# Taking the dummy products out between the last four modes of a spectral-mixing kernel

## Chip, cores, metric

One core of a Trainium2 chip. The metric is the device time of one execution in microseconds (us). All timed runs below count as fast in the record. Where runs of one kernel are called long, they are the longer ones among these.

## The reference

Sliding-window causal attention, then a spectral mix of its output along the sequence, then a channel product with a rectifier:

```python
attn_out = _attn_ref(q, k, v)               # 8 batches, 8 heads, 576 rows, 64 wide, window 64
X = np.fft.rfft(x, axis=1)                  # x: (8, 576, 512)
Yr = einsum(Xr, w_r) - einsum(Xi, w_i)      # 64 modes, a 512x512 matrix for each
Yi = einsum(Xr, w_i) + einsum(Xi, w_r)
y = np.fft.irfft(Y, n=S, axis=1)
u = x + y
out = u + np.maximum(u @ w_ch, 0.0)
```

The weights w_r and w_i, 128 matrices of 512x512, are most of what is read.

## The kernel before

The weights stream in, one matrix (512 KB as bf16) every 2.45 us, and TensorE multiplies each as it lands. The last four modes (ME = 60 to 63) are done in a narrow form, `last`, 16 columns wide. Their result `psl` is copied, turned into rows (`turned`: four 512-column products and four transposes), and then the 36 output tiles are made: `lay(n)` puts a first product into the bank of tile n, `rectify(n)` adds a second and applies the rectifier on ScalarE, `finish(n)` adds the third and hands the tile to VectorE. Between the last groups stand dummy products, `idle`, into a bank that nobody reads:

```python
def idle(wide, n):
    psd = ps_a.tile([128, DM], FP32, name="psd", tag="psw")
    for _ in range(wide):        # fp32 128x512: two products in the trace (x10 for five)
        nc.tensor.matmul(out=psd, lhsT=ident_r.bitcast(FP32), rhs=Z0[:, 0, :].bitcast(FP32), start=True, stop=True)
    for _ in range(5 * n):       # bf16, 96 columns
        nc.tensor.matmul(out=psd[:, 0:96], lhsT=ident_bf, rhs=view(x_sb, 0, [[1, 96]]), start=True, stop=True)

def last_mode(m, w, im, c0, c1):             # 16 weight loads, 16 products of 16 columns
    for c in range(c0, c1):
        for e in range(NC):
            nc.tensor.matmul(out=view(psl, ...), lhsT=w[:, c, 128*e:128*e+128], rhs=xq(c, m, im, ...), ...)

# ... (TensorE in program order)
last(ME + 1, 0)
for n in range(2, EARLY_ROWS):
    lay(n)
idle(1, 0)
last(ME + 1, 1)
for m in range(ME + 2, NM):
    for im in range(2):
        idle(1, 2)
        last(m, im)
idle(0, 2)
# ... the turn of the last rows
nc.vector.tensor_copy(out=view(YT2, ...), in_=view(psl, ...))
nc.vector.tensor_copy(out=YT2[:, :, 2 * R:], in_=psl[:, :, 2 * RL:])
turned(lambda e: YT2[:, e, 0:NR], NR, psa, psw)
lay(EARLY_ROWS)
# ... copies of psa and psw; then rectify(n), finish(n), lay(n) for 36 tiles, stores
turn_of = {1: 3, 5: 4, 9: 5, 12: 6, 15: 7}   # when the late rows of a batch are sent (Y <- yl)
```

The softmax here doesn't subtract the row's maximum and nothing guards it: scores larger than these inputs give would overflow.

## Time and profile before

| | before |
|---|---|
| time, median of the first 3 runs | 426.87 us (426.59 to 426.88) |
| span of the profiled run | 424.8 us |
| last group of narrow products starts | 390.05 us |
| turn of the last rows, four 512-column products | 1.17 us |
| first store of output issued | 396.81 us |
| TensorE clock in the seam, 380 to 395 us | 1.00 |

All places in time are us from the start of the span. The weights' DMA sets the time up to 390 us; then comes a short serial seam; the first output leaves at 397 us, and from 398 us the output runs with DMA, TensorE and ScalarE full and VectorE nearly so (400 to 410 us: DMA 0.98, the engines 10.00, 10.00 and 9.36 us busy). The prediction shows the lines. In them PE is TensorE, PEld its weight loads, DVE VectorE, ACT ScalarE and POOL GpSimd; L724 is line 724 of the kernel, and x4 counts instructions.

### The profile page before, as it was taken

To read this page: it belongs to the slowest core of one execution; us is meant where nothing else is said; L and a number is where in the kernel's file an instruction comes from. 1 tells how busy PE (TensorE), PEld (TensorE's weight loads), DVE (VectorE), ACT (ScalarE), POOL (GpSimd) and SP (SyncE) were. 2 spreads that over 40 slices of the span, in tenths; PEclk is the share of its full clock that TensorE was granted. 3 is DMA by queue.
4 is the path that set the end of the run, shared out by engine and by line. 5 is a ranking of instruction groups with operands and counts; after the bars stand their busy time and mean duration, and the time that the engine had idled before them with its cause. 6 is when DMAs were issued, how large, how long until landed. Compare 5 with 4: busy or idle time off the path is not lost.

```text
span 424.8 us, 8859 instructions
## 1 busy us (share of the span) xinstructions
PE 360.5 (85%) x3762; PEld 219.2 (52%) x3772; DVE 184.7 (43%) x397; ACT 171.4 (40%) x314; POOL 89.5 (21%) x171
## 2 busy tenths in 40 slices
PE   6989998998998899467698979999859886589993
PEld 5755765665665465222265646555334443256682
DVE  5566766766764201404542422333113432140994
ACT  4585765866863311201132313122113332130993
POOL 7231231331021141221221121121211032200000
PEclk9999999999995699965799998999999999999998
DMA  8999999999999999999999999999999999994598
GB/s 144 212 213 212 213 213 212 213 213 213 213 214 213 215 213 261 213 214 213 214 213 214 213 214 214 213 215 212 214 213 213 214 213 215 213 214 95 195 384 329
DMA packets 28646, 91.98 MB, mean 217 GB/s; under 512 B 2832, under 2 KB 3088, under 8 KB 28608
## 3 DMA queue, kind: packets, MB, share of 16 engines
q0 software_dynamic: 25344, 81.80, 96.6%
q1 hardware_dynamic: 3120, 9.50, 5.8%
q8 instruction: 29, 0.48, 0.4%
q10 hardware_dynamic: 144, 0.13, 0.1%
q14 instruction: 9, 0.07, 0.0%
HBM read 162.53 MB, written 9.44 MB: 405 GB/s over the span
## 4 chain that ended last, share of the span: by engine, by line
DMA 45%; PE 40%; DVE 8%; issue 2%; ACT 2%; POOL 1%; DVEq 0%; POOLq 0%
DMA wt<-in_moe_w_r_dram 32%; DMA wt<-in_moe_w_i_dram 9%; PE pso L316 7%; PE psy L575 7%; PE pst L218 6%; DMA wy<-in_moe_w_i_dram 5%; PE pso L885 4%; PE psv L235 3%; DVE x_sb L324 3%; PE psx L338 3%; PE pss L371 3%; PE pss L272 2%; PE pss L291 2%; DVE vT L59 2%; PE psw L724 1%
## 5 line engine op out<-in xcount | busy, mean ns | idle before, releaser
L575 PE MATMUL psy<-wt,XQ 128*32 128x512 bf16 (+1 forms) x404 | 96.6, 409 | 30.8 <-DMA wt<-in_moe_w_i_dram 15.5
L575 PEld LDWEIGHTS <-XQ 128*32 128x32 bf16 x476 | 48.6, 131 | 76.5 <-issue 57.0
L604 DVE CAST xT<-pxt 128x256 fp32r<-128x256 bf16 (+1 forms) x68 | 26.3, 434 | 53.8 <-PE pxt L597 34.1
L115 POOL DMA_DIRECT2D wt<-in_moe_w_r_dram x54 | 28.9, 536 | 92.2 <-DMA wt<-in_moe_w_r_dram 39.9
L611 ACT CAST Z<-psz 128x512 fp32r<-128x512 f32 x36 | 21.1, 586 | 66.6 <-PE psz L609 66.5
L115 POOL DMA_DIRECT2D wt<-in_moe_w_i_dram x52 | 28.0, 539 | 82.0 <-DMA wt<-in_moe_w_i_dram 43.7
L297 ACT ACTIVATE et<-pss 128x512 bf16<-128x512 f32 x72 | 39.2, 600 | 13.5 <-PE pss L291 13.4
L609 PE MATMUL psz<-wch,xT 128*128 128x512 f32 x144 | 42.4, 432 | 0.9 <-DVE xT L604 0.9
L316 PE MATMUL pso<-vt,et 128*64 128x65 bf16 (+1 forms) x576 | 34.3, 210 | 4.8 <-DVE x_sb L324 4.7
L609 PEld LDWEIGHTS psz<-wch,xT 128*128 128x128 f32 x144 | 27.1, 200 | 15.0 <-issue 8.7
L316 PEld LDWEIGHTS <-et 128*64 128x64 bf16 (+1 forms) x576 | 24.0, 114 | 17.1 <-issue 9.6
L59 DVE COPY x_sb<-psy 128x256 f32<-128x256 f32 x15 | 6.4, 424 | 56.7 <-PE psy L575 56.7
L324 DVE TENSOR_TENSOR x_sb<-pso,rcp 128x640 bf16<-128x640 f32 x32 | 26.3, 823 | 0.9
L58 ACT COPY x_sb<-psy 128x256 f32<-128x256 f32 x15 | 5.6, 373 | 50.2 <-DVE x_sb L59 50.2
L885 PE MATMUL pso<-Y,trigI 128*128 128x512 f32 x80 | 23.1, 402 | 0.1
L908 DVE TENSOR_TENSOR ot<-pso,x_sb 128x512 f32<-128x512 f32 x35 | 22.2, 685 | 1.5 <-PE pso L885 1.1
L272 PE MATMUL pss<-band,ident_bf 64*64 64x512 bf16 x136 | 20.6, 414 | 1.5 <-ACT et L297 1.5
L59 DVE CAST x_sb<-psj 128x512 bf16<-128x512 f32 x18 | 12.2, 688 | 21.3 <-PE psj L786 18.3
L59 DVE COPY vT<-pst 128x768 bf16<-128x768 bf16 x16 | 15.3, 958 | 13.0 <-PE pst L218 13.0
L890 ACT ACTIVATE pso<-pso 128x512 f32<-128x512 f32 x36 | 19.2, 597 | 0.0
L58 ACT CAST x_sb<-psj 128x512 bf16<-128x512 f32 x18 | 10.5, 585 | 19.6 <-PE psj L786 19.6
L291 PE MATMUL pss<-qT,kT 64*64 64x128 bf16 (+1 forms) x640 | 17.3, 221 | 0.3 <-issue 0.3
(157 smaller groups left out, 501.3 us busy)
## 6 DMA issues: line engine op xcount, KB each, us to landing
wt<-in_moe_w_r_dram POOLq DMA_DIRECT2D x54, 512.0 KB, 19.1
wt<-in_moe_w_i_dram POOLq DMA_DIRECT2D x52, 512.0 KB, 19.1
out_dram<-ot SPq DMA_DIRECT2D x15, 512.0 KB, 4.2
rk<-in_k_dram POOLq DMA_DIRECT2D x8, 576.0 KB, 9.7
rq<-in_q_dram POOLq DMA_DIRECT2D x8, 576.0 KB, 13.6
rv<-in_v_dram POOLq DMA_DIRECT2D x8, 576.0 KB, 12.3
wy<-in_moe_w_r_dram POOLq DMA_DIRECT2D x3, 512.0 KB, 17.7
wy<-in_moe_w_i_dram POOLq DMA_DIRECT2D x3, 512.0 KB, 19.1
```

Source lines behind the costliest of these rows:

```text
L59: return nc.vector.tensor_copy(out=o, in_=i)
L115: nc.gpsimd.dma_start(out=wt, in_=src[m].rearrange("(p c) e -> p c e", c=NC))
L218: nc.tensor.transpose(out=ps[64 * hh:64 * hh + 64, c, :], in_=src[:, hh, (c0 + c) * D:(c0 + c + 1) * D], identity=ident_bf)
L272: nc.tensor.matmul(out=pss[(2 * w + hh) % 3][64 * half:64 * half + 64, :], lhsT=ident_bf[pp, pp], rhs=view(band[pp], 128 * half, [[0, WIN ...
L291: nc.tensor.matmul(out=pss[(2 * w + hh) % 3][64 * half:64 * half + 64, col:col + nq], lhsT=kTs[b % 2][pp, g, 64 * kb:64 * kb + 64], rhs=qT ...
L297: nc.scalar.activation(out=et[:, hh, :], in_=pss[(2 * w + hh) % 3], func=ACT_F.Exp, scale=EX_SCALE)
L316: nc.tensor.matmul(out=pso[po, hh, (i // 2) * VW:(i // 2) * VW + D + 1], lhsT=et[pk, hh, col:col + 64], rhs=vt[pk, 1 - f % 2, 2 * hh + g / ...
L324: nc.vector.tensor_tensor(out=view(x_sb, b * NT * DM + g * D, [[4 * D, 2], [DM, NT], [1, D]]), in0=view(pso, 0, [[512, 2], [VW, NT], [1, D]]),
L575: nc.tensor.matmul(out=psy[r0:r0 + k, :], lhsT=xq(c, m, im, [[NM, k]]), rhs=w[:, c, :], start=(im + c == 0), stop=(im == (m > 0) and c == ...
L604: nc.vector.tensor_copy(out=xT[:, :, w * k:w * k + w], in_=view(psts[k], j, [[128, NC], [n, w]] if n > 1 else [[128, NC], [1, 64], [64, 2]]))
L609: nc.tensor.matmul(out=psz, lhsT=xT[:, c, :], rhs=wch[:, c, :], start=(c == 0), stop=(c == NC - 1))
L885: nc.tensor.matmul(out=tps[n], lhsT=trigI[:, tr:tr + 128], rhs=pair_tile(what, bb), start=False, stop=stop and r0 + k == 128, skip_group_c ...
```

## The change

Its intent, as the diff shows it: no dummy work between the last modes, as TensorE waits for weights there anyway, and only five small dummies where there were ten, in the turn.

```diff
         for n in range(2, EARLY_ROWS):
             lay(n)
-        idle(1, 0)
         last(ME + 1, 1)
         for m in range(ME + 2, NM):
             for im in range(2):
-                idle(1, 2)
                 last(m, im)
-        idle(0, 2)
+        idle(0, 1)
```

## The prediction

> **What bounds the kernel now.** I read the page first, for the rhythm of the whole run. The rows below have 40 slices of 10.6 us each. The first is the TensorE clock that was granted, the second the DMA share.

> ```profile
> PEclk9999999999995699965799998999999999999998
> DMA  8999999999999999999999999999999999994598
> ```

> The DMA engines are full until slice 36 (382 us); in that time the kernel loads weights, and TensorE has time to spare. Slices 37 and 38 (382 to 403 us) are the seam, where the weights are over and the output has not begun; after it the DMA is full again with output. A change in the seam can cost time, and this change lies just there. Next I read the chain of waits that ended last, in order of time (start, length, what):

> ```profile
> 370.83 19.17 DMA wy<-in_moe_w_i_dram
> 390.00 0.05 issue
> 390.05 0.67 PE psl L775 x16
> 390.71 0.02 issue
> 390.74 0.23 DVE YT L862
> 390.96 0.28 DVE YT L864
> 391.24 0.14 issue
> 391.37 1.17 PE psw L724 x4
> 392.54 0.02 issue
> 392.56 0.58 ACT Y L877
> 393.14 0.04 issue
> 393.19 2.19 PE pso L885 x7
> ```

> The last weights land at 390.00. From then on everything is in series: 16 narrow products of the last mode, two copies on VectorE, the turn of the last rows (four 512-column products), a copy on ScalarE, and then the output tiles, TensorE being named almost without a break. No dummy product (L739, L741) stands in this chain. The timeline shows the same from the side of TensorE; the bracket is the idle time before, and what ended it:

> ```profile
> 387.55 0.65 PE L775 MATMUL psl<-XQ,wy 128*128 128x16 bf16 x16 [0.25 <-DMA wy<-in_moe_w_r_dram]
> ...
> 390.05 0.65 PE L775 MATMUL psl<-XQ,wy 128*128 128x16 bf16 x16 [0.48 <-DMA wy<-in_moe_w_i_dram]
> ...
> 391.34 0.73 PEld L724 LDWEIGHTS psw<-wch,YT 128*112 128x112 f32 x4 [0.37 <-PE psd L741]
> ```

> The dummies ahead of the last two groups were done before the weights came. The third line names a dummy (psd) as releaser, but the last dummy ended at 391.13 and the VectorE copy L864 at 391.23, so the copy is what the turn really waited for. After 393 us no engine has slack to take up a delay:

> ```profile
> 400.00:410.00 10.00, 10.00 (x45) 8.01 (x44) 9.36 (x15) 10.00 (x21) 0.00 (x0) 1.00 0.98 378
> ```

> TensorE (second number), VectorE, ScalarE and DMA (0.98 at 378 GB/s) are all full. What is lost before 397 us, where the first output leaves, should come out at the end.

> **The clock.** What the dummies can be good for is the clock. Its changes in this trace lie on a grid: falls and rises at 128.0, 145.1, 179.2, 186.0, 189.4, 199.7, 206.5, 213.3, 254.3, 257.7, 370.4, 373.8 and 421.6 us are all multiples of 3.413 us apart. I therefore asked for the busy time of stretches cut on that grid (length, then TensorE busy with its count, and after the other engines the clock):

> ```profile
> 186.04:189.45 3.41, 1.49 (x6) 0.52 (x5) 0.00 (x0) 0.00 (x0) 0.53 (x1) 1.00 1.05 211
> 206.52:209.93 3.41, 2.30 (x6) 0.63 (x6) 2.06 (x7) 0.40 (x2) 0.53 (x1) 0.50 1.06 214
> 312.33:315.75 3.42, 1.70 (x9) 0.79 (x7) 0.68 (x2) 0.37 (x1) 0.62 (x2) 1.00 1.05 211
> 366.95:370.36 3.41, 1.09 (x7) 0.63 (x6) 0.69 (x1) 0.58 (x1) 0.53 (x1) 1.00 1.06 213
> 370.36:373.77 3.41, 2.89 (x8) 1.00 (x7) 0.42 (x1) 0.37 (x1) 0.53 (x1) 0.50 1.05 211
> ...
> 387.43:390.84 3.41, 2.81 (x52) 2.10 (x53) 0.10 (x1) 0.00 (x0) 0.00 (x0) 1.00 0.21 42
> ```

> [...]Here four 512-column bf16 products took 1.86 us at half clock (209.50) and 1.02 us at full (363.00); and single 128x512 fp32r products last 632 ns at half clock (L609, 210 to 213 us) against 409 ns.

> **The change, part by part.**
> 1. Removed: five wide dummies (ten array passes in the trace, 5.4 us busy) and 45 of the 50 narrow ones (2.9 us x 45/50 = 2.6 us). That is 8.0 us of busy TensorE between 380.6 and 391.1, all beside DMA waits. The reordering comparison shows only these go; every other engine keeps its order, and no load is issued later than 370.83. Gain on the path: 0.
> 2. What is left between 381 and 390 us is a group of 16 narrow products, 0.63 us, each time weights land, every 2.45 us. A grid stretch then has at most two groups, 1.3 us, and one that has one group has 0.6 us; both are under the 1.6 us limit. So the clock falls at 384.0 or 387.4, and in any phase TensorE is at half clock when the last weights land at 390.0.
> 3. What half clock costs on the chain. Last group of 16: 0.65 us, [...]no such group ran at half clock, so I estimate +0.4. Turn of the last rows: three steps of 0.427[...] and a last one of 0.632 make 1.91 us instead of 1.17, +0.74. First output product: its 0.40 becomes 0.63, but it was 0.14 us ahead of ScalarE's own second copy (end 393.73), so only about +0.1 counts. VectorE and ScalarE do not change. Sum up to the first rectified tile: about +1.2 us. The five narrow dummies that stay take some 0.4 us at half clock and lie beside the VectorE copies: 0.
> 4. From there each output tile needs three 512-column products of TensorE, 0.69 us at full and 1.28 us at half clock, against about 0.65 us of ScalarE. As long as the clock stays down, half of the time that passes is lost.
> 5. When it comes back. The seam from 390.05 on is mostly busy, with a hole for the copies. A window needs about 2.8 of its 3.41 us busy. If narrow products count fully, windows that start at 389.6 or later suffice; if they hardly count, from 391.0. So the rise comes between 393.0 and 397.8, by phase; middle 395.4. In the chain at half clock, output products start about 394.3. Loss: 1.2 + (395.4 - 394.3)/2 = 1.75 us; about 1 with an early rise, 2.9 with a late one.
> 6. Through to the end: all engines are full after 397, so the delay passes on, apart from a little that small gaps of the DMA take up. I carry 1.75 us over.

> 426.87 + 1.75 = 428.6 us.

> **Rivals.**
> *Dummies worth nothing.* If the clock did not fall, or rose before the turn, the time would stay at 426.8. For it: a rise by 393.0 would save some of the chain. Against it: 1.3 us busy at most per window, and falls with 1.49 us.
> *Dummies in the way.* If they held up a landed group, their removal would gain up to 0.6 us (426.3). Against: both last groups waited for the DMA, and the turn waited for VectorE.
> *Output DMA hides it.* If writing were bound by its own rate, an early loss would still count, as writing starts later by it. Only if the first tiles leave on time would it vanish; then 427.2. The first store is issued at 396.81, after the whole slow part, so this is weak.
> *Clock stays down for two windows.* If the blurred limit is missed twice, to about 400 us, the loss is 1.2 + 5.7/2 = 4.0 us, 430.9. Against: the output products leave no holes.

> **Range and chances.** The phase alone spans 427.8 to 429.8; rival one and three stretch it down, rival four up: 427.3 to 429.9. Two per cent is 8.5 us, twice my worst case, and no gain reaches it: faster 0.005, same 0.985, slower 0.01.

> **What would show it.** The clock should read 0.50 from 384 or 387 us to somewhere in 393 to 398. The last group should still wait for weights at 390.0, its 16 products take about 1.05 us and the turn 1.9 us; the first store should be issued 1 to 3 us after 396.81, and the span after that be as long as before. A clock at 1.00 through the seam, or a span after the first store that is shorter by the delay, would prove me wrong.

0.4 + 0.74 + 0.1 is about 1.2 us, and (395.4 - 394.3)/2 = 0.55 makes it 1.75. The 0.427 us are in the trace of the kernel before: at half clock, bf16 products of 512 columns start at 209.88, 210.30 and 210.73; three such steps are the 1.28 us of step 4. The +0.4 was a guess with no measurement behind it. The limits of 1.6 and 2.8 us are estimates from the stretches quoted, there and in the expectations below. That the grid can lie otherwise against 390 us in another execution was assumed, and first shown by the runs below. That VectorE and ScalarE do not change is shown by the profiles of the changed kernel: at half clock the two VectorE copies take 0.22 and 0.28 us (0.23 and 0.28 before), and three tiles on ScalarE 1.56 us, as before.

## The result, and the profile after

428.06 us, median of 4 runs (427.96 to 428.29), against 426.74 us (426.59 to 426.88, 4 runs). The ratio is 1.0032, 95% interval 1.0014 to 1.0049. Here and below, a ratio is the mean time of one kernel's runs over that of the other's of the same rounds, so not quite the ratio of the medians. A cost of 0.3%: within 2%, and clear of noise.

The slices of the page, as in the prediction (a slice is now 10.7 us):

```profile
PEclk9999999999995899656699999999999999895997
DMA  8999999999999999999999999999999999993598
```

The clock has a new dip in slice 37 (383.7 to 394.3 us), where it stood at 9. (The dips further left, in the time that the weights' DMA sets, lie a little differently in the two profiles and cost nothing that shows at 390 us.) The chain of waits through the seam (start, length, what):

```profile
390.00 0.69 PE psl L775 x16
390.72 0.22 DVE YT L860
390.94 0.28 DVE YT L862
391.22 0.14 issue
391.35 2.02 PE psw L724 x4
393.37 0.43 PE psa L726 x4
393.80 0.54 PE pso L769
394.34 1.93 PE pso L883 x7
```

The last group starts at the same time as before. The turn takes 2.02 us in place of 1.17. Two pieces are new in the chain: the transposes and the laying of the sixth tile, which at half clock last longer than the ScalarE copy beside them (0.43 + 0.54 us against 0.58). By the timeline the first output product starts 0.96 us later than before (394.15 against 393.19; the chain enters it at 394.34, as products overlap), and the first seven end 0.89 us later (396.27 against 395.38). Stretches cut on the grid of clock changes (length; busy time and count of PE, PEld, DVE, ACT and POOL; clock; DMA share and GB/s):

```profile
380.55:383.96 3.41, 1.41 (x34) 1.02 (x32) 0.49 (x1) 0.00 (x0) 0.00 (x0) 1.00 1.07 216
383.96:387.37 3.41, 0.66 (x16) 0.55 (x16) 0.00 (x0) 0.00 (x0) 0.00 (x0) 0.50 0.75 149
387.37:390.79 3.42, 1.45 (x36) 1.34 (x37) 0.07 (x1) 0.00 (x0) 0.00 (x0) 0.50 0.25 49
390.79:394.20 3.41, 3.14 (x14) 2.18 (x12) 0.78 (x3) 0.77 (x2) 0.00 (x0) 0.50 0.00 0
```

The first stretch has 1.41 us busy and the next runs at half clock. The clock is back at 394.20, after a stretch with 3.14 us. The first store is issued at 397.70, 0.89 us later than before. In mid-output there is one more wait, which the kernel before has not:

```profile
412.31 0.19 PEld L883 LDWEIGHTS pso<-Y,trigI 128*128 128x128 f32 x1 [0.38 <-DMA Y<-yl]
```

A product needs late rows that a small transfer has not brought yet; there the delay of the chain grows from 0.87 us (411.60 against 410.73) to 1.13 us (414.19 against 413.06). The last DMA of the core ends 1.41 us later (424.78 against 423.37), and the span is 1.4 us longer.

### The profile page after: what moved, and what is told of

Read it like the earlier page. It is cut to its first block, busy times and chain, and to the rows that moved or that the text cites. A ratio compares the mean times of both kernels' runs of the same rounds, so it can differ in the third digit from the quotient of the medians.

```text
span 426.3 us, 8748 instructions
## 1 busy us (share of the span) xinstructions
PE 357.0 (84%) x3707; PEld 216.8 (51%) x3717; DVE 184.5 (43%) x397; ACT 171.4 (40%) x314; POOL 89.3 (21%) x171
## 4 chain that ended last, share of the span: by engine, by line
DMA 52%; PE 34%; DVE 7%; issue 2%; ACT 2%; POOL 1%; DVEq 0%; POOLq 0%
DMA wt<-in_moe_w_r_dram 32%; DMA wt<-in_moe_w_i_dram 9%; PE pso L316 6%; PE pst L218 6%; DMA wch<-in_moe_w_ch_dram 5%; DMA wy<-in_moe_w_i_dram 5%; PE pso L883 4%; PE psv L235 3%; DMA qT<-in_moe_w_i_dram 3%; DVE x_sb L324 3%; PE pss L371 2%; PE pss L272 2%; PE psy L575 2%; PE psx L338 2%; PE pss L291 2%
## 5 line engine op out<-in xcount | busy, mean ns | idle before, releaser
L575 PE MATMUL psy<-wt,XQ 128*32 128x512 bf16 (+1 forms) x404 | 98.9, 416 | 29.8 <-DMA wt<-in_moe_w_i_dram 16.1
L609 PE MATMUL psz<-wch,xT 128*128 128x512 f32 x144 | 42.5, 432 | 0.9 <-DVE xT L604 0.9
L609 PEld LDWEIGHTS psz<-wch,xT 128*128 128x128 f32 x144 | 27.1, 200 | 15.0 <-issue 8.7
L883 PEld LDWEIGHTS pso<-Y,trigI 128*128 128x128 f32 x80 | 14.6, 188 | 5.5 <-ACT pso L888 1.6
```

Source lines behind the costliest of these rows:

```text
L575: nc.tensor.matmul(out=psy[r0:r0 + k, :], lhsT=xq(c, m, im, [[NM, k]]), rhs=w[:, c, :], start=(im + c == 0), stop=(im == (m > 0) and c == ...
L609: nc.tensor.matmul(out=psz, lhsT=xT[:, c, :], rhs=wch[:, c, :], start=(c == 0), stop=(c == NC - 1))
L883: nc.tensor.matmul(out=tps[n], lhsT=trigI[:, tr:tr + 128], rhs=pair_tile(what, bb), start=False, stop=stop and r0 + k == 128, skip_group_c ...
```

## The experiments

Theory: the dummies do one thing, they keep the clock up, and what counts is the clock in the turn. Rivals: TensorE must be kept busy through all the late modes; the dummies act otherwise (order, waits); the late wait for Y<-yl is part of the cost. The kernel before was run 11 times beside the first four experiments (426.57 us, 426.45 to 427.56) and those runs with one more (12 runs, 426.55 us) serve the later ones.

**One gap filled.** The changed kernel with four bf16 dummies of 512 columns ahead of the very last group only:

```diff
             for im in range(2):
+                if (m, im) == (NM - 1, 1):
+                    psd = ps_a.tile([128, DM], FP32, name="psd", tag="psw")
+                    for _ in range(4):
+                        nc.tensor.matmul(out=psd, lhsT=ident_bf, rhs=view(x_sb, 0, [[1, DM]]), start=True, stop=True)
                 last(m, im)
```

> The changed kernel with four 512-column bf16 dummies in one place only, the gap ahead of the very last group of 16 narrow products. The clock theory: the clock still falls at 384.0 us as in the changed kernel, but the stretch 387.4 to 390.8 now holds 0.66 + 1.75 + 0.68 = about 3.1 us of work, over the 2.8 us limit, so the clock is back at 390.8, ahead of the turn; the time is that of the kernel before, 426.7 us (0.1 either way). Rival (what counts is a TensorE kept busy through all the late modes, or something else in the removed dummies): 428.0 us as in the changed kernel.

427.57 us (427.42 to 428.32), ratio 1.0024 (1.0012 to 1.0036): the expectation of 426.7 fell. Its stretches:

```profile
383.53:386.94 3.41, 0.65 (x16) 0.53 (x16) 0.00 (x0) 0.00 (x0) 0.00 (x0) 1.00 0.82 166
386.94:390.36 3.42, 2.81 (x34) 1.36 (x35) 0.00 (x0) 0.00 (x0) 0.00 (x0) 0.50 0.28 56
390.36:393.77 3.41, 3.14 (x23) 2.37 (x19) 0.49 (x3) 0.43 (x1) 0.00 (x0) 0.50 0.00 0
```

The grid lay 0.43 us earlier than in the profile that I had reckoned with, and the stretch that should have brought the clock back held 2.81 us, not 3.1: not enough. The turn ran at half clock (2.02 us). So the run did not test the theory; it showed that the phase of the grid can be another in another execution, and that 2.81 us were too little to come back there.

**Without the five small ones.** `-        idle(0, 1)` in the changed kernel.

> The changed kernel without the five small dummies that it kept in the turn of the last rows. If those five carry weight for the clock, the stretch 390.8 to 394.2 drops from 3.1 us busy to about 2.8, at the limit: with a miss the rise moves from 394.2 to 397.6 us, 3.4 us more of output products run at half clock, and the time is about 1.7 us longer, 429.7 us. Rival (the five are without effect, since the four 512-column products fill the stretch): 428.06 us, the rise at 394.2 as before. I hold both for about equally likely.

427.95 us (427.80 to 428.51), ratio 1.0034 (1.0021 to 1.0047), the same as the changed kernel (428.06; 428.19 in its second series). The five have no effect that these runs can see.

**Narrow or wide ones alone.** Two versions of the kernel before:

```diff
 # narrow only                         # wide only
-        idle(1, 0)                             idle(1, 0)
-                idle(1, 2)            -                idle(1, 2)
+                idle(0, 2)            +                idle(1, 0)
         idle(0, 2)                    -        idle(0, 2)
```

> The kernel before with all narrow dummies kept and the five wide ones taken away. By the busy-time limits: each burst is 0.62 + 0.5 = 1.1 us every 2.45 us; the stretch 384.0 to 387.4 holds one burst, 1.1 us, under the 1.6 us limit, so the clock falls at 387.4, and the next stretch with 1.9 us does not bring it back: half clock in the turn, 428.0 us as the changed kernel. Rival (any dummies keep the clock): 426.7 us.

> The kernel before with only the five wide dummies, all narrow ones taken away, the ten at the turn too. By the busy-time limits each burst is 0.63 + 1.1 = 1.7 us every 2.45 us, every stretch holds at least 2.0 us, over the 1.6 us limit: the clock stays at 1.00 and the time is 426.7 us. Rival (the narrow ones, or those at the turn, are needed): 428.0 us.

Narrow only: 427.83 us (427.59 to 429.32), ratio 1.0032 (1.0019 to 1.0044), as the changed kernel. Wide only: median 426.69 us, as the kernel before in four of six runs, but 428.28 and 429.00 in two; ratio 1.0014 (0.9995 to 1.0032). The stretch of each with the least work in the seam (narrow only first, wide only second; they are two profiles):

```profile
381.81:385.22 3.41, 1.05 (x26) 0.91 (x26) 0.00 (x0) 0.00 (x0) 0.00 (x0) 1.00 1.05 210
```
```profile
386.24:389.65 3.41, 1.99 (x19) 0.77 (x18) 0.00 (x0) 0.00 (x0) 0.00 (x0) 1.00 0.41 82
```

After 1.05 us the clock fell and stayed down until 395.46; after 1.99 us it stayed up. So not any dummy will do. This also speaks against the second rival: the narrow-only kernel has dummies in four of the five places, in the same bank, and costs what the changed kernel costs. The wide ones add more busy time, but busy time as the profile counts it is not the whole measure. A stretch of the kernel without the small ones held no less and was followed by half clock, from 381.71 us on:

```profile
378.29:381.71 3.42, 2.08 (x39) 1.47 (x36) 1.37 (x2) 0.98 (x2) 0.00 (x0) 1.00 1.06 213
```

It has 32 narrow products, four transposes and three 512-column products. What else counts was not tested. The profile of the wide-only kernel is of one of its short runs; why two of its runs were long was not seen.

**Two gaps filled.** As the first experiment, but mended against the phase:

```diff
             for im in range(2):
+                if m == NM - 1:
+                    busy(4)          # four bf16 dummies of 512 columns
                 last(m, im)
```

> The changed kernel with four 512-column bf16 dummies in each of the last two gaps (ahead of the last two groups), the remedy for the first experiment, whose single gap missed a whole clock stretch by its phase. Here TensorE is busy almost without a break from 385.0 to 390.7 us, 5.7 us even at half clock, so a stretch of 3.41 us ending between 387.9 and 391.3 holds at least 2.8 us busy whatever the phase. The clock theory: the clock may fall after 383 us and is back by the turn at 391.3; first store at 397.2 and time 426.6 us, as the kernel before. Rival (the dummies must run through all the late modes, or do something other than keep the clock): 427.5 to 428.1 us, as the changed kernel.

426.76 us (426.73 to 427.07, 4 runs), ratio 1.0004 (0.9989 to 1.0018): as the kernel before. Its stretches:

```profile
382.27:385.68 3.41, 1.32 (x33) 1.10 (x34) 0.00 (x0) 0.00 (x0) 0.00 (x0) 0.50 1.00 201
385.68:389.09 3.41, 3.29 (x23) 1.17 (x22) 0.00 (x0) 0.00 (x0) 0.00 (x0) 0.50 0.49 97
389.09:392.51 3.42, 2.52 (x31) 1.71 (x30) 0.49 (x2) 0.05 (x1) 0.00 (x0) 1.00 0.02 4
```

The clock was down from 382.3 to 389.1 us, through three of the late groups, and back before the turn, which took 1.17 us in the chain and this in the timeline (start, length, ...):

```profile
391.26 1.16 PE L724 MATMUL psw<-wch,YT 128*112 128x512 f32 x4 [0.46 <-DVE YT L869]
```

The first store left at 396.72. This decides between the theory and its first rival: half clock in the late modes cost nothing here; the cost comes with half clock in the turn and after it. In this profile, too, one product waited for Y<-yl (0.3 us), so that wait isn't peculiar to the change.

**Late rows sent earlier.** In the changed kernel:

```diff
-        turn_of = {1: 3, 5: 4, 9: 5, 12: 6, 15: 7}
+        turn_of = {1: 3, 3: 4, 5: 5, 7: 6, 9: 7}
```

> The changed kernel with the small transfers of late rows (Y from yl) issued earlier among the stores (after tiles 1, 3, 5, 7, 9 in place of 1, 5, 9, 12, 15). In the profile of the changed kernel one output product waited 0.38 us for such a transfer at 412.3 us, and the delay grew from 0.87 to 1.14 us there. If that wait is a part of the cost of the change: 427.8 us, 0.25 less than the changed kernel. Rival (the wait is chance or is replaced by another, as the stores are behind by then): the same as the changed kernel of this call, within 0.1 us.

428.67 us (427.94 to 431.11, 6 runs), ratio 1.0060 (1.0039 to 1.0082). The wait is not in the profile, but no run is shorter than 427.94 us, where the changed kernel's shortest was 427.95, and four runs are longer than 428.2 us. The expectation fell. What makes those runs long was not seen.

**The changed kernel again**, on the same chip as the last two and the dense version:

> The changed kernel itself again, on the same chip as the other three, as their measure: 427.5 to 428.3 us. The clock falls between 381 and 387.4 us and rises between 393 and 396 us, at a phase of its own; the turn takes 2.0 us and the first store leaves 0.9 to 1.4 us later than in the kernel before.

428.19 us (427.95 to 428.47, 4 runs), ratio 1.0035 (1.0022 to 1.0048). Its profile has no wait for Y<-yl at all, and a span of 426.2 us, near the 426.3 of the first: the cost is there without that wait. Its clock was later to come back, at 396.49:

```profile
391.23 2.02 PE psw L724 x4
...
394.23 2.74 PE pso L883 x7
```

The turn is the same, and the first seven output products now take 2.74 us in the chain (1.93 with the rise at 394.20). Now six profiles of the seam at half clock can be set side by side, with times counted from the start of the last group, to take out small shifts of the load:

| kernel | clock back after | first store after | later than before's 6.76 |
|---|---|---|---|
| one gap | 3.83 us | 7.66 us | 0.90 |
| changed | 4.20 | 7.70 | 0.94 |
| no small | 5.44 | 7.88 | 1.12 |
| narrow only | 5.49 | 8.09 | 1.33 |
| sends early | 5.67 | 7.93 | 1.17 |
| changed again | 6.61 | 8.21 | 1.45 |

For the three versions with the clock up in the turn (wide only, two gaps, dense) the first store comes after 6.77, 6.78 and 6.78 us. At least 0.9 us are lost in all six, and from the first row to the last another 0.2 us for each us that the clock stays down: (1.45 - 0.90)/(6.61 - 3.83). That is a mean of two rows, not an even slope. In the first five rows the store is issued as soon as SyncE has issued the small transfer of late rows ahead of it (0.8 us); in the last it waits for VectorE's second output tile, which ends at 398.06. The narrow-only kernel lies 0.2 us above the no-small one of the same phase: in its chain its ten dummies at half clock stand ahead of the turn, which starts 1.49 us after the last group (1.30 without the small ones), so there they were in the way.

**Dense dummies.** Seven of the 512-column ones ahead of each of the last five groups:

```diff
+        busy(7)
         last(ME + 1, 1)
         for m in range(ME + 2, NM):
             for im in range(2):
+                busy(7)
                 last(m, im)
```

> The changed kernel with seven 512-column bf16 dummies ahead of each of the last five groups: denser than the kernel before. At full clock one burst is 1.7 + 0.6 = 2.3 us of the 2.45 us between weights, so no stretch comes near the 1.6 us limit. Clock theory: 1.00 through the seam in every phase, 426.5 us with less scatter than the kernel before. If dense dummies get in the way of a landed group, up to 0.3 us longer; if the clock is down on entry in some run, they overrun the gap (3.0 us each) and that run is about 2 us longer.

427.28 us in the median, of two kinds: three runs at 426.55 to 426.57, three at 427.98 to 428.60; ratio 1.0017 (1.0000 to 1.0033). The profiled run was of the short kind. To see the long kind, the same kernel was looked at three times more:

> The dense kernel once more, for a profile of its slow kind: three of its six runs took 428.0 to 428.6 us, three 426.55. Theory: in the slow ones the clock is down when TensorE enters the seam at 380.7 us; seven dummies then take 3.0 us and a burst 3.6 us of the 2.45 us between weights, so a group that has landed starts late, and the lateness is still there at the last group, which then starts 1 us or more after its weights at 389.9. In a fast one the clock is 1.00 from before 380 us and the last group waits for its weights. Rival: the slow ones show the clock down in the turn (391 to 394 us) with the last group on time.

> The same look again, as the phase of the clock can't be chosen: a fast run shows 1.00 on entry to the seam, a slow one 0.50 on entry and a last group of narrow products that starts late, by as much as the run is longer (1.4 to 2 us). Rival: clock down in the turn.

> The same look a third time: a fast run shows 1.00 on entry to the seam, a slow one 0.50 on entry and a late last group. Rival: clock down in the turn. With half of the runs slow, one of the three looks should be slow with a chance of about 7 in 8.

426.70, 428.11 and 427.48 us (single looks, state unknown). The timeline of the first, a short one, and of the second, a long one (start, length, engine, what): the dummies ahead of the fifth-last group, the last group, and in the first also the turn.

```profile
379.60 1.69 PE L746 MATMUL psd<-x_sb,ident_bf 128*128 128x512 bf16 x7
...
389.93 0.65 PE L780 MATMUL psl<-XQ,wy 128*128 128x16 bf16 x16 [0.31 <-DMA wy<-in_moe_w_i_dram]
...
391.26 1.15 PE L724 MATMUL psw<-wch,YT 128*112 128x512 f32 x4 [0.46 <-DVE YT L869]
```
```profile
382.12 1.69 PE L746 MATMUL psd<-x_sb,ident_bf 128*128 128x512 bf16 x7
...
391.52 0.63 PE L780 MATMUL psl<-XQ,wy 128*128 128x16 bf16 x16
```

In the long one the clock was down from 370.2 to 380.4 us, ahead of the seam (up from 315 us on in the short one). TensorE reached the seam 2.5 us late, and each burst of dummies and group takes 1.98 us of the 2.45 between weights, so it could make up too little: the last group started at 391.52, 1.6 us late and without waiting for weights. The third look lies between (clock down from 370.5 to 377.3, last group 0.9 us late). So the lateness was as expected and the turn was at full clock; but its origin was not the one that I wrote: the dummies themselves ran at full clock (1.69 us for seven, not the 3.0 of seven steps of 0.427). They only left no room to catch up.

## Why the prediction was right, point by point

- *What bounds the kernel; the gain of the removal is 0.* Held. The last group started at 390.00 against 390.05.
- *The clock falls at 384.0 or 387.4 and is down at 390.0.* Held: it fell at 383.96 (382.83 in the second profile), and it was down when the last weights landed in both. The limit near 1.6 us, from which this was worked out, is not general. Stretches with 1.05 and 1.41 us fell and one with 1.99 did not, but one with 2.08 fell. The prediction had read its limits only where weights are loaded; its own list of changes begins with a fall at 128.0 us, after a stretch with 2.57 us busy (124.60 to 128.01), nearly all short attention products.
- *Cost on the chain, +1.2 us.* The mechanism was right, the terms were not. The turn was put at +0.74 and measured +0.85 (2.02 against 1.17). The group of 16 narrow products was put at +0.4 and measured +0.02 (0.69 against 0.67 in the chain, not the 1.05 us named as a sign): its weight loads took 108 ns each against 98, and it hardly slowed. The first output product was put at +0.1; here the clock came back just after it had started, and in the second profile ScalarE waited 0.29 us for it. Counted from the start of the last group, the first tile is rectified 0.93 us later than before here and 1.15 us later in the second profile. So the sum of 1.2 came out nearly right by luck: the group that was put too high stood in for the parts that were put too low.
- *From there half of the time is lost.* This step was mis-sized: 0.2 us for each us, not 0.5. The first three tiles on ScalarE, in the kernel before and in the second profile of the changed one, which was at half clock until 396.49:

```profile
393.76 1.56 ACT L890 ACTIVATE pso<-pso 128x512 f32<-128x512 f32 x3
394.74 1.56 ACT L888 ACTIVATE pso<-pso 128x512 f32<-128x512 f32 x3 [0.29 <-PE pso L883]
```

They start late, but take no longer. The step counted three products for each tile, 1.28 us at half clock. But these tiles were laid earlier, and the program does the `rectify` products of five tiles first: one for each, some 0.43 us apart at half clock (394.50, 394.93, 395.35), where ScalarE starts a tile every 0.49 us at either clock. What is lost beyond that shows later, on VectorE, which waits 0.96 us for the first finished tile in the second profile.
- *The clock comes back between 393.0 and 397.8.* Held in all six profiles (393.77 to 396.49). The limit of 2.8 us for coming back is not sharp: 2.81 us (one gap) and 2.92 us (389.66 to 393.07 in the changed kernel's second profile) did not do, 2.89 us before the seam and 3.14 us did.
- *The delay passes on to the end.* Held in part: 0.89 us at the first store, 1.13 at the last products, 1.41 at the last DMA in the first profile, and 1.3 to 1.6 us in the medians. Two more of the signs that the prediction named failed in this profile: the first store was to leave 1 to 3 us late, and the rest of the span was to be as long as before (28.57 us against 28.03). In the second profile both held (1.28 us, and 28.09). The wait for Y<-yl accounts for the step from 0.87 to 1.13 in the first profile; in the second there is none and the later clock takes its place. What adds the last 0.3 us behind the last product was not tested.
- *Rivals.* That dummies are worth nothing fell by the result, and so did the output that hides it (427.2): the first store was late. That they are in the way fell too, at the size used before; with seven wide ones per gap it came true in some runs. A clock that stays down to 400 us was not seen.

The point of 428.6 us was 0.5 us too long, within the range of 427.3 to 429.9. The half of the time from step 4 was too much, and what came on behind the first store made up for part of it, so that it lies as near as this is in part luck.

## What to carry to other kernels

Work that looks idle may hold up the TensorE clock (1.00 in the seam with the dummies here, 0.50 from 383.96 to 394.20 us in the profile without the 8.0 us that were taken out); before taking it out, cut the trace on the grid of clock changes and ask which stretches would be left with little work, and which part of the chain then runs at half clock. No single limit in busy time held here, so look at the clock in the trace afterwards. It was enough that the clock was back where TensorE is on the path (here the turn). So fill the time just ahead of that, with long products (here 512 columns) and for longer than one stretch (3.41 us), since the phase differed between executions. Leave slack between the dummies: in one look (state unknown), bursts of 1.98 us in the 2.45 us between weights left the last group 1.6 us late, of the 2.5 us that TensorE was late on entry.

## What these traces show of the clock

- Busy time alone did not decide it. Stretches of 3.41 us that were far from idle were followed by half clock: with 1.55 us busy in the kernel before (250.89), 2.08 without the small dummies, and 2.57 among short attention products (124.60), where one with 1.70 (312.33) and one with 1.99 (wide only) were not. At half clock, 2.92 us did not bring it back in one run, nor 3.23 in the attention stage (134.84 to 138.25), and 2.89 and 3.14 did.
- No long gap was needed. The clock fell after a stretch of the kernel before with no gap longer than 1.43 us (366.95 to 370.36), and stayed down in the changed one with groups of 0.66 us every 2.45 us.
- The phase of the grid differed between executions. In the two profiles of the changed kernel the clock was back 4.20 and 6.61 us after the last group started. It is easy to be misled, all the same: the first profiles of the two kernels agreed in phase to 0.05 us (370.36 against 370.31), so one pair of profiles can make the phase look fixed. The traces of this one-core kernel show clocks of 1.00 and 0.50 alone.
- A group of 16 weight loads (128x128 bf16) with products of 16 columns took 0.61 to 0.67 us at full and 0.63 to 0.68 us at half clock in the late modes: these groups are all but untouched by it. The prediction put 0.4 us there.
